# Gated attention mix: projection products split into two 64-row halves that run beside the scores

## The chip, the cores and the metric

The kernel runs on one core of a Trainium2 chip. The metric is device time in microseconds (us), from the start to the end of the program on that core. TensorE appears as PE in the profile (PEld is its weight load), VectorE as DVE, ScalarE as ACT, GpSimd as POOL, SyncE as SP. A bank is one of the eight PSUM areas of 128x512 float32 into which PE writes and from which ACT and DVE read.

## The reference, cut to what matters

Two attention blocks A and B share the input x of 2048x640 and differ in their weights. Their results are mixed row by row with a gate.

```python
def block(x, wqkv, wo):                       # S=2048, D=640, H=32 heads of Dh=20
    qkv = (x @ wqkv).reshape(B, S, 3, H, Dh).transpose(2, 0, 3, 1, 4)
    q, k, v = qkv
    p = softmax(einsum("bhqd,bhkd->bhqk", q, k) * Dh ** -0.5)
    o = einsum("bhqk,bhkd->bhqd", p, v)
    return o.transpose(0, 2, 1, 3).reshape(B, S, D) @ wo

g = sigmoid((x * gate_w).sum(-1, keepdims=True))
out = g * block(x, A_wqkv, A_wo) + (1 - g) * block(x, B_wqkv, B_wo)
```

## The kernel before

The heads are taken four at a time: 8 groups of block A, then 8 of block B, so 16 groups, numbered 0 to 15. In a group the 2048 queries go in four blocks of 512, and the 2048 keys in eight pairs of tiles of 128. One **step** is one query block against two key tiles for four heads; there are 16 x 4 x 8 = 512 steps (`STEPS`). Every matrix product of float32 data is done as three float16 products of a high and a low part (`wh`, `wl`, `xh`, `xl`).

What PE does in a step:

- **Scores** (`scores`, line 632): 8 matmuls of 64 rows by 512 columns. Head pairs sit in rows 0 to 63 (`j` = 0, in the order `e0`) and 64 to 127 (`e1`), so two scores of different halves run side by side. ACT takes each score's exponential out of its bank (line 635).
- **Maxima** (`max_mm`, line 574): 8 matmuls of the same size, transposed (`m0`, `m1`), for a query block to come, up to `LEAD` = 15 steps ahead. DVE reduces them to row maxima (line 585); for some, ACT first takes a Relu of one bank (line 578) and DVE joins it with a second (line 582). The scores of a query block can only start when its maxima are done, since the maximum is an operand row of the score.
- **Values** (`values`, line 650): twice a step four float32 matmuls of 128 rows, one per head, into the bank `acc` in strips of 32 columns. The order calls them `V`.
- **Products** (`mms`, line 375), called `X`: pieces of the projections of later groups (`project_a`, `project_r`: queries and keys; `project_v`: values), of the output projection (`out_tiles`) and of its last part (`last_tiles`, line 813). A piece is mostly 15 matmuls of 128 rows and 160 to 176 columns into one bank, which ACT (lines 402, 530, 715) or DVE (line 717) then takes out.

There are seven banks for scores, maxima and products. `take` gives the bank that is expected to be free first, `give` says when, with a clock kept at build time (`clock`, `rows_free`, `free_at`). On each engine the instructions run in the order in which the build writes them.

The order of a step is a text, picked by how late the products are: `STEP[0]` without a product, `STEP[1]` with one, `STEP[2]` with two, and `LATE` where no maxima are left. Products wait in the list `fill` with the step from which they may be done and the step by which they are due; `behind` compares the two, `slot` does one piece. Where a query block's maxima are not ready when its step comes, a loop does further maxima and pieces until they are. After the last step a second loop finishes what is left.

Of the kernel before, what the change touches and what calls it, by code (L numbers as in the profile page):

```python
# [31 lines left out]
NS = 8  # L32
# [29 lines left out]
def kernel(  # L62
# [73 lines left out]

    def tick_score(j, i):
# [230 lines left out]
    def mms(i, out_ap, pairs, cost):  # L368

        if now[0] >= 0:  # L370
            tick_block(len(pairs) * cost * T_SCORE, free_at[i])
        for k, (a, b) in enumerate(pairs):
            if now[0] < 0:
                tick_block(cost * T_SCORE, free_at[i])
            nc.tensor.matmul(out_ap, a, b, start=(k == 0), stop=(k == len(pairs) - 1))  # L375
            if now[0] < 0:
                yield
# [6 lines left out]
    def project_chunk(w, hi, lo, ch):  # L384
# [9 lines left out]
        if now[0] >= 0:  # L394
            f = work.tile([P, QB], F32, name="fs")
            for k in range(3):
                if k:
                    yield
# [4 lines left out]
                give(i, spend("act", 0.25, clock["done"]))  # L403
# [115 lines left out]
    def project_v(gg, j):  # L519
# [3 lines left out]
        for u in range(2):  # L523
            if u and now[0] >= 0:
                yield
            n = slice((j + u) * P, (j + u + 1) * P)
            i, pt = take()
            yield from mms(i, pt[:, :w], [(a[:, c, n], b[:, c, :w]) for c in range(NC) for a, b in
                                          ((xh, wh), (xh, wl), (xl, wh))], 0.33)
# [155 lines left out]
    def out_tiles(job, t, state):  # L685
# [17 lines left out]
        def products():  # L703
            wh, wl = wo_parts[z]
            for k in range(0, D, width):
                if k:
                    yield
                n = slice(k, k + width)
                i, pt = take()
                yield from mms(i, pt[:, :width], [(o[:p, a, c - c0], w[:p, c, n])  # L710
                                                  for c in range(c0, c1) for p in (P if c < full else 48,)
                                                  for a, w in ((0, wh), (0, wl), (1, wh))], width / QB)
# [17 lines left out]
        soon(state["due"], D // width, products())  # L730
# [71 lines left out]
    def last_tiles(qb, o):  # L802
        wh, wl = wo_parts[2]
        for t in range(4):
            c = slice(t * P, (t + 1) * P)
            f = f_o[1][:, 4 * qb + t:4 * qb + t + 1]
            for half in range(2):
                n = slice(half * 320, half * 320 + 320)
                y = y_sum[:, 4 * qb + t, n]
                i, pt = take()  # L810
                tick_block(0.4, free_at[i])
                for k, (a, w) in enumerate(((0, wh), (0, wl), (1, wh))):
                    nc.tensor.matmul(pt[:, :320], o[:, a, c], w[:, n], start=(k == 0), stop=(k == 2))  # L813
# [9 lines left out]
            yield  # L823
# [160 lines left out]
    for g in range(2 * NG):  # L984
        b = g * NQ * NS
        n = g + 1
        if n < 2 * NG:
            fill += [(b - 8, b + 4 + ch, 3, project_a(n, ch)) for ch in range(4)]
# [3 lines left out]
            if i < 4:  # L992
# [7 lines left out]
                if g % 4 == 3:  # L1000
                    fill += [(b - 9, b + 4 + ch, 3, project_r(i, ch)) for ch in range(4)]
            gg = g // 2 + 1
            if gg < NG and g % 2 == 0:
# [4 lines left out]
                fill += [(b + 10, b + 14 + 3 * j, 2, project_v(gg, j)) for j in range(0, NT, 2)]  # L1008
# [13 lines left out]
    outs = [(NG * step + 2 + int(9 * t), jobs[0], t) for t in range(NT)]  # L1022
# [9 lines left out]
    def out_tasks(G):  # L1032
# [8 lines left out]
        if last and all(4 * last[0][0] + t in summed for t in range(4)):  # L1041
            soon(now[0] + 6, 4, last_tiles(*last.pop(0)))

    def behind(G):

        n = sum(f[0] for f in current)
        for f in sorted((f for f in fill if f[0] <= G), key=lambda f: f[1]):
            n += f[2]
            if n > max(1, f[1] - G):
                return True  # L1050
        return False

    def slot(G):
        if not current:
            able = [f for f in fill if f[0] <= G]
            if not able:
                return
            first = min(able, key=lambda f: f[1])
            fill.remove(first)
            current.append([first[2], first[3]])  # L1060
        try:
            next(current[0][1])
            current[0][0] -= 1
        except StopIteration:
            current.clear()
# [37 lines left out]
    for G in range(STEPS + 1):  # L1103
        g, qb, i = unit_of(G)
        now[0] = G
        while G < STEPS and ((g, qb) not in ready or (G and not valued(G - 1))):
            for u, ch in next_maxima(G, 1):
                for j in (1, 0):
                    one_max(u, ch, j)
# [3 lines left out]
            slot(G)  # L1113
        some = next_maxima(G, 4)
        blocks = 0 if not current and not any(f[0] <= G for f in fill) else 2 if behind(G) else 1
        count = {}
        for what in (STEP[blocks] if maxima or some else LATE + " X" * (blocks == 2)).split():
            k = count[what] = count.get(what, 0) + 1
            if what[0] == "e":
                q = sum(count.get(f"e{j}", 0) for j in range(2)) - 1  # L1120
                j = int(what[1])
                if G < STEPS:
                    scores(G, (k - 1) // 2, (k - 1) % 2, (j,))
# [6 lines left out]
            elif what[0] == "m":  # L1130
                for u, ch in some[(k - 1) * len(some) // 4:k * len(some) // 4]:
                    one_max(u, ch, int(what[1]))
            elif what == "V":
                product()
                if G:
                    values(G - 1, k - 1)
                    if G % NS == 0 and k == 2 and G < STEPS:
                        side.append(take_acc(*unit_of(G - 1)[:2]))
                        advance()
            else:  # L1140
                slot(G)
# [35 lines left out]
```

## Time and profile before

| | |
|---|---|
| Time, median of 3 runs (lowest to highest) | 2835.39 us (2834.82 to 2835.52) |
| Span of the profiled execution, first to last instruction | 2832.8 us |
| Time around the span (median less span) | 2.6 us |
| PE, DVE, ACT busy | 2773.1, 2443.8, 2529.7 us |
| PE's granted clock, mean | 0.996 |
| Chain that ended last, share of PE | 91% |

The profiled execution has no time of its own beside its span, so the median of the runs less the span stands for what lies around it. Matmuls are recorded from start to the arrival of their result, so two that follow each other overlap in the records: how long a matmul keeps PE is read from the distance between two starts.

### The profile page before, as it was taken

The page shows a single profiled execution, that of the slowest core. Times are in us where ns is not written, and L with a number is a line of the kernel's source. Part 1 is how long each engine was busy: PE and PEld are TensorE (multiplying, and loading weights), DVE is VectorE, ACT ScalarE, POOL GpSimd, SP SyncE. Part 2 cuts the span into 40 slices and gives each one's busy share as a digit, 9 for nine tenths or more (in the row PEclk, how much of TensorE's full clock was granted, in tenths as well). Part 3 has the DMA queues.
Part 4 walks back from the last instruction along what each step waited for, and adds up shares of the span by engine and source line. Part 5 has one row for each costly group of instructions (what it writes and reads, how often), then busy time and mean ns, then how long its engine had stood idle before and what let it go on. Part 6 is the DMA issues. An engine that isn't in the chain of part 4 may idle for free.

```text
span 2832.8 us, 62443 instructions
## 1 busy us (share of the span) xinstructions
PE 2773.1 (98%) x23362; PEld 970.8 (34%) x23362; DVE 2443.8 (86%) x4763; ACT 2529.7 (89%) x5122; POOL 671.8 (24%) x914
## 2 busy tenths in 40 slices
PE   6999999999999999999999999999999999999998
PEld 3533223342323323343233333334333333332222
DVE  6688999879999898988989888887888989989982
ACT  3799999989999999989999999998899999888887
POOL 5312113231221212233431111222112233120011
PEclk9999999999999999999999999999999999999999
DMA  4110101001020101202021020211202112122222
GB/s 135 35 45 7 39 6 42 16 16 29 13 52 16 37 11 27 47 13 50 17 56 44 14 60 16 48 37 24 49 15 61 38 38 70 55 71 60 63 60 74
DMA packets 167170, 113.71 MB, mean 40 GB/s; under 512 B 102224, under 2 KB 140808, under 8 KB 166864
## 3 DMA queue, kind: packets, MB, share of 16 engines
q1 hardware_dynamic: 164320, 108.09, 15.6%
q8 instruction: 183, 3.00, 0.4%
q0 software_dynamic: 1600, 0.96, 0.2%
q14 instruction: 123, 1.01, 0.1%
q10 hardware_dynamic: 944, 0.66, 0.1%
HBM read 48.89 MB, written 26.61 MB: 27 GB/s over the span
## 4 chain that ended last, share of the span: by engine, by line
PE 91%; DVE 5%; ACT 1%; DMA 1%; POOL 1%; issue 1%; SPq 0%; POOLq 0%; DVEq 0%; ACTq 0%
PE acc L650 34%; PE bank L375 20%; PE bank L632 19%; PE bank L574 17%; DVE mpart L585 3%; ACT pt L635 1%; DVE rl L582 1%; DMA xs<-in_A_x_dram 0%; ACT rl L578 0%; DMA wv<-in_A_wqkv_dram 0%; DVE ot L736 0%; PE bank L813 0%; PE bank L183 0%; PE bank L862 0%; DVE wmax L227 0%
## 5 line engine op out<-in xcount | busy, mean ns | idle before, releaser
L635 ACT ACTIVATE pt<-bank 128x512 f32<-128x512 f32 x4096 | 2157.5, 614 | 155.0 <-PE bank L632 75.1
L585 DVE TENSOR_REDUCE mpart<-bank 128x1 f32<-128x512 f32 x2976 | 1867.8, 681 | 264.3 <-PE bank L574 167.1
L650 PE MATMUL acc<-pt,v 128*21 128x512 f32 x8192 | 1082.0, 600 | 3.4 <-DVE ot L736 3.1
L632 PE MATMUL bank<-qt,kt 64*128 64x512 f16 x4096 | 1056.3, 380 | 11.9 <-ACT pt L635 4.5
L574 PE MATMUL bank<-kt,qt 60*128 60x512 f16 x3536 | 1013.0, 380 | 4.0 <-DVE mpart L585 0.7
L574 PEld LDWEIGHTS <-qt 60*128 60x128 f16 x4096 | 235.4, 94 | 686.6 <-issue 629.0
L632 PEld LDWEIGHTS <-kt 64*128 64x128 f16 x4096 | 248.1, 94 | 456.7 <-issue 322.8
L582 DVE CUSTOM_DVE_ANT_0 rl<-bank,rl 128x512 f32<-128x512 f32 x560 | 377.5, 678 | 20.5 <-ACT rl L578 8.2
L578 ACT ACTIVATE rl<-bank 128x512 f32<-128x512 f32 x560 | 329.8, 595 | 14.6 <-PE bank L574 12.3
L744 POOL TENSOR_TENSOR ot<-ot,sq 128x512 f32<-128x512 f32 x63 | 66.0, 1047 | 993.0 <-DVE sq L741 993.0
L650 PEld LDWEIGHTS acc<-pt,v 128*21 128x21 f32 x8192 | 143.0, 99 | 434.6 <-issue 421.5
L375 PE MATMUL bank<-xx,wbh 128*128 128x168 f16 (+2 forms) x2240 | 280.1, 244 | 3.2 <-ACT xx L866 1.9
L375 PE MATMUL bank<-xx,wbl 128*128 128x168 f16 (+2 forms) x1120 | 252.8, 243 | 0.0
L375 PEld LDWEIGHTS <-wbh 128*128 128x128 f16 x2240 | 183.6, 98 | 86.8 <-issue 79.8
L574 PE MATMUL bank<-kd,qt 60*128 60x512 f16 x560 | 203.6, 381 | 1.7 <-DMA kd<-dd 1.2
L375 PE MATMUL bank<-wvh,xx 128*128 128x160 f16 (+1 forms) x1280 | 155.4, 234 | 0.5 <-ACT pt L635 0.3
L375 PE MATMUL bank<-woh,o_in 128*128 128x160 f16 (+1 forms) x960 | 155.7, 256 | 0.0
L375 PEld LDWEIGHTS <-xx 128*128 128x128 f16 x1920 | 131.6, 97 | 52.7 <-issue 49.4
L404 POOL CAST cq<-fs 128x512 f16<-128x512 f32 x60 | 36.6, 609 | 446.0 <-ACT fs L402 444.0
L375 PE MATMUL bank<-wvl,xx 128*128 128x160 f16 (+1 forms) x640 | 137.3, 231 | 0.6 <-POOL wvl L315 0.6
L375 PEld LDWEIGHTS <-o_in 128*128 128x128 f16 (+1 forms) x1440 | 104.0, 97 | 75.3 <-issue 62.2
L402 ACT ACTIVATE fs<-bank 128x168 f32<-128x168 f32 (+1 forms) x216 | 67.5, 313 | 56.6 <-PE bank L375 40.0
(131 smaller groups left out, 1305.2 us busy)
## 6 DMA issues: line engine op xcount, KB each, us to landing
y_scr<-y_out SPq DMA_DIRECT2D x32, 320.0 KB
kt<-cq SPq DMA_DIRECT2D x120, 80.0 KB
o_scr<-on SPq DMA_DIRECT2D x240, 40.0 KB
kt<-cq SPq DMA_DIRECT2D x136, 40.0 KB
xs<-in_A_x_dram SPq DMA_DIRECT2D x8, 640.0 KB
o_in<-o_scr SPq DMA_DIRECT2D x32, 160.0 KB
y_out<-y_scr SPq DMA_DIRECT2D x16, 320.0 KB
xx<-y_scr SPq DMA_DIRECT2D x16, 320.0 KB
```

The costliest lines, as they stand in the source:

```text
L375: nc.tensor.matmul(out_ap, a, b, start=(k == 0), stop=(k == len(pairs) - 1))
L402: nc.scalar.activation(f[:, m], pt[:, m], AF.Copy, scale=QKS)
L404: nc.gpsimd.tensor_copy(hi, f)
L574: nc.tensor.matmul(pt, QT[g % 2][r, pair, q0:q0 + P], k, start=True, stop=True)
L578: nc.scalar.activation(relus[u, j], pt, AF.Relu)
L582: nc.vector.tensor_tensor_reduce(rl, pt, rl, 1.0, LOW, OP.add, OP.max, m)
L585: nc.vector.tensor_reduce(m, pt, axis=AX.X, op=OP.max)
L632: nc.tensor.matmul(et, KT[g % 2][r, pair, kt * P:(kt + 1) * P], QT[g % 2][r, pair, qb * QB:(qb + 1) * QB], start=True, stop=True)
L635: nc.scalar.activation(pt, et, AF.Exp, scale=factor(g // 4))
L650: nc.tensor.matmul(acc[32 * h:32 * h + VW, :], V[(g // 2) % 2][:, kt, (g % 2) * GH + h, :], ptiles.pop((G, kk, h)), start=(kt == 0), stop= ...
L744: nc.gpsimd.tensor_tensor(t3, t3, sq.unsqueeze(2).to_broadcast([P, 16, 32]), op=OP.mult)
```

## The change

Products are no longer blocks of 128-row matmuls. `halves_of` writes each matmul as two of 64 rows: first all those on rows 0 to 63, then all those on rows 64 to 127, accumulating in the same bank. While a half runs on one set of rows, the scores and maxima of the other rows are written between its matmuls. The second half of a product may begin only when a wait that PE has already made proves that the first half's writes have landed (`seen`, `synced`, `wrote`); up to two products may be open at once (`limit=2`).

The order of a step is no longer a text. A loop writes scores and maxima in turn, and half matmuls where `wanted` allows them. `pace` sets how much product time a step may take, between `PACE` = 1.9 and `HASTE` = 3.4 us counted for one half (the old order could do two whole pieces). The values stand where 6/16 and 14/16 of the step's scores and maxima have been written. In the waiting loop and after the last step, `alone` does up to 15 products a turn as 128-row blocks (`solo`). The output tiles of the first job come every 6.2 steps instead of every 9.

```diff
-STEP = ("e0 m1 V e1 m0 e0 m1 e1 m0 e0 m1 e1 m0 V e0 m1 e1 m0",
-        "X e0 m1 m0 e1 m0 m1 V m1 e0 e1 m0 e1 e0 V m0 e1 e0 m1",
-        "X m0 m1 e0 m1 e0 e1 V e1 e0 m1 m0 V e1 m0 m1 m0 e0 e1 X")
-LATE = "e0 e1 e0 e1 V X e0 e1 e0 e1 V"
+COLUMN = 1 / 2400
+CHUNK = 30 * QB * COLUMN
+PACE, HASTE = 1.9, 3.4
...
+    def halves_of(width, pairs):
+        todo = [(r, slice(64 * r, min(64 * r + 64, a.shape[0])), a, b) for r in range(2) for a, b in pairs
+                if a.shape[0] > 64 * r]
+        cost = width * COLUMN + 0.003
+        i = pt = None
+        for k, (r, rows, a, b) in enumerate(todo):
+            turned = k > 0 and todo[k - 1][0] != r
+            yield r, cost, len(todo) * cost if k == 0 else 0, count[0] if turned else 0
+            if k == 0:
+                i, pt = take()
+                seen(i)
+                if solo[0]:
...
+                    return i, pt
...
+            nc.tensor.matmul(pt[:, :width], a[rows], b[rows], start=(k == 0), stop=(k == len(todo) - 1))
...
-            for k in range(3):
-                if k:
-                    yield
+            for k in range(len(PARTS) - 1):
                 m = slice(PARTS[k], PARTS[k + 1])
-                i, pt = take()
-                yield from mms(i, pt[:, m], pairs(slice(t0 + m.start, t0 + m.stop)), 0.34)
-                nc.scalar.activation(f[:, m], pt[:, m], AF.Copy, scale=QKS)
+                n = m.stop - m.start
+                i, pt = yield from halves_of(n, pairs(slice(t0 + m.start, t0 + m.stop)))
+                nc.scalar.activation(f[:, m], pt[:, :n], AF.Copy, scale=QKS)
...
-    outs = [(NG * step + 2 + int(9 * t), jobs[0], t) for t in range(NT)]
+    outs = [(NG * step + 2 + int(6.2 * t) + (45 if t > 12 else 0), jobs[0], t) for t in range(NT)]
...
+    def pace(G):
+        n, most = float(len(current)), PACE
+        for f in sorted((f for f in fill if f[0] <= G), key=lambda f: f[1]):
+            n += f[2]
+            most = max(most, 1.1 * n / max(1, f[1] - G))
+        return min(most, HASTE)
+
+    def wanted(G, limit=2, free=False):
+        for x in current:
+            if x[1][3] <= synced[0] and (x[1][2] == 0 or free or credit[0] > 0.0):
+                return x
+        while len(current) < limit and (free or credit[0] > 0.0):
...
         while G < STEPS and ((g, qb) not in ready or (G and not valued(G - 1))):
...
-            slot(G)
+            for _ in range(15):
+                alone(G)
...
+        v_at = [6 * total // 16, 14 * total // 16] if maxima or some else [total // 2, total]
...
+            r = x[1][0]
...
+            if not emit_s(1 - r):
+                emit_s(r)
+                continue
+            while True:
+                x = wanted(G)
+                if x is None or x[1][0] != r or rows_free[r] + 0.5 * x[1][1] > rows_free[1 - r]:
+                    break
+                emit_x(x)
```

**A step in the middle, on PE.** First the order before, from one `V` (line 650) to the next. L574 is a maximum, L632 a score, L375 a product's matmul; `bank0` to `bank6` are the seven banks, and "waits" names the engine whose reading of that bank must have ended.

```order
L650 MATMUL acc_88<-pt_15398,v1_87 21x512
L574 LDWEIGHTS qt1_81
L574 MATMUL bank6_95<-kt1_83,qt1_81 128x512 [waits DVE_49]
...
L632 MATMUL bank3_92<-qt0_80,kt0_82 128x512 [waits Activation_49]
...
L632 MATMUL bank4_93<-qt0_80,kt0_82 128x512 [waits DVE_49]
L574 LDWEIGHTS qt1_81
L574 MATMUL bank0_89<-kt1_83,qt1_81 128x512 [waits Activation_49]
L375 LDWEIGHTS xx_79
L375 MATMUL bank1_90<-wvh_14700,xx_79 128x160 [waits DVE_49]
...
L632 LDWEIGHTS kt0_82
L632 MATMUL bank5_94<-qt0_80,kt0_82 128x512 [waits Activation_49]
```

The product's 15 matmuls stand together, with four scores and maxima between the values and the product. Now the same stretch after the change, again from one values block to the next (L666 is a score, L608 a maximum, L410 a half matmul, L684 the values); between the rows shown stand three L410 matmuls each time, all into `bank1`.

```order
L684 MATMUL acc_88<-pt_18882,v1_87 21x512
L666 LDWEIGHTS kt1_83
L666 MATMUL bank4_93<-qt1_81,kt1_83 128x512 [waits DVE_49]
...
L608 MATMUL bank2_91<-kt1_83,qt1_81 128x512 [waits Activation_49]
...
L666 MATMUL bank0_89<-qt1_81,kt1_83 128x512 [waits Activation_49]
...
L608 MATMUL bank3_92<-kd1_85,qt1_81 128x512 [waits DVE_49]
...
L666 MATMUL bank6_95<-qt1_81,kt1_83 128x512 [waits DVE_49]
...
L608 MATMUL bank4_93<-kt1_83,qt1_81 128x512 [waits Activation_49]
...
L666 MATMUL bank0_89<-qt1_81,kt1_83 128x512 [waits Activation_49]
...
L608 MATMUL bank2_91<-kt1_83,qt1_81 128x512 [waits DVE_49]
...
L410 MATMUL bank3_92<-xx_79,wbh_17719 128x176 [waits Activation_49]
L684 MATMUL acc_88<-pt_18907,v1_87 21x512
```

Eight scores and maxima now stand between two values blocks, and `bank4`, `bank0` and `bank2` are each written twice within the stretch, while `bank1` and `bank5` hold open products. The first three rows are all on rows 0 to 63; the product's matmuls are on rows 64 to 127.

**The end of group 11, on PE.** Before the change the maxima of group 12 (L574, `qt0`) stand among the scores of group 11 (L632, `qt1`) throughout:

```order
L574 LDWEIGHTS qt0_80
L574 MATMUL bank2_91<-kt0_82,qt0_80 128x512 [waits DVE_49]
L632 LDWEIGHTS kt1_83
L632 MATMUL bank1_90<-qt1_81,kt1_83 128x512 [waits Activation_49]
L632 LDWEIGHTS kt1_83
L632 MATMUL bank4_93<-qt1_81,kt1_83 128x512 [waits DVE_49]
L574 LDWEIGHTS qt0_80
L574 MATMUL bank5_94<-kt0_82,qt0_80 128x512 [waits Activation_49]
```

After the change the last 13 steps of the group hold no maximum, and at its last step the waiting loop writes two 1-column matmuls (L1133), 30 half matmuls, then 315 product matmuls in one piece (L402, here its end), then the maxima of group 12 (L608):

```order
L402 MATMUL bank5_94<-wol_19690,o_in_32472 128x160
L402 LDWEIGHTS o_in_32472
L402 MATMUL bank5_94<-woh_19689,o_in_32472 128x160
L608 LDWEIGHTS qt0_80
L608 MATMUL bank6_95<-kd0_84,qt0_80 128x512 [waits Activation_49]
L608 LDWEIGHTS qt0_80 [waits DMAHW4_49,DMAHW3_49]
L608 MATMUL bank0_89<-kt0_82,qt0_80 128x512 [waits Activation_49]
```

In that place 95 maxima follow each other before the next score.

**After the last values block, on PE.** Before the change the four small L777 to L788 steps are followed by the last 24 matmuls of `last_tiles` (L813). After it, 129 further 320-column matmuls (L402) of output tiles that the steps had not reached stand between the two.

More of the change, by code (lines that the diff above doesn't have):

```diff
@@ L1058, in slot, with follow @@
             first = min(able, key=lambda f: f[1])
             fill.remove(first)
[L1060 to L1065, printed above, removed]
+            x = [first[3], None]
+            if follow(x):
+                return x
+        return None
+    def follow(x):
+        x[1] = next(x[0], None)
+        if x[1] is None:
+            if x in current:
+                current.remove(x)
+            return False
+        if x not in current:
+            current.append(x)
+        return True
@@ new lines, in emit_x, with alone @@
+    def emit_x(x):
+        credit[0] -= x[1][2]
+        follow(x)
+    def alone(G):
+        x = wanted(G, 1, True)
+        if x is None and current:
+            i, pt = take()
+            mark = wts.tile([P, 1], F32, name="m1", tag="m1", bufs=2)
+            for n in range(2):
+                tick_block(0.1, free_at[i])
+                seen(i)
+                nc.tensor.matmul(pt[:, :1], KT[1][:, 0, :P], KT[1][:, 0, :1], start=True, stop=True)
+                if n == 0:
+                    nc.vector.tensor_copy(mark, pt[:, :1])
+                    free_at[i] = spend("dve", 0.1, clock["done"])
+            give(i, clock["done"])
+        elif x is not None:
+            solo[0] = True
+            emit_x(x)
+            solo[0] = False
@@ L1145 @@
         product()
-        slot(STEPS)
+        for _ in range(15):
+            alone(STEPS)
         out_tasks(STEPS)
```

150 lines of the change are left out of this document (94 added, 56 removed).

## The prediction

> **What bounds the kernel now.** I read the page's head and its chain of waits first.
>
> ```profile
> span 2832.8 us, 62443 instructions
> PE 2773.1 (98%) x23362; PEld 970.8 (34%) x23362; DVE 2443.8 (86%) x4763; ACT 2529.7 (89%) x5122; POOL 671.8 (24%) x914
> PE 91%; DVE 5%; ACT 1%; DMA 1%; POOL 1%; issue 1%; SPq 0%; POOLq 0%; DVEq 0%; ACTq 0%
> ```
>
> PE sets the end, but ACT and DVE are close behind, so what a step costs depends on its mix. The timeline of PE shows a step with one product:
>
> ```profile
> 1441.50 1.06 PE L650 MATMUL acc<-pt,v 128*21 128x512 f32 x8
> 1442.49 0.39 PE L574 MATMUL bank<-kt,qt 60*128 60x512 f16 x1
> 1442.49 0.60 PE L632 MATMUL bank<-qt,kt 64*128 64x512 f16 x2
> 1442.72 0.38 PE L574 MATMUL bank<-kt,qt 60*128 60x512 f16 x1
> 1443.03 0.32 PE L375 MATMUL bank<-xx,wbh 128*128 128x168 f16 x2
> ...
> 1444.06 0.24 PE L375 MATMUL bank<-xx,wbl 128*128 128x168 f16 x1
> 1444.22 0.39 PE L632 MATMUL bank<-qt,kt 64*128 64x512 f16 x1
> ...
> 1448.26 0.32 PE L375 MATMUL bank<-xx,wbh 128*128 128x168 f16 x2
> ```
>
> Starts are what count. A pair of scores comes every 0.22 us; the product's 15 matmuls every 0.073 us (1443.03 to 1444.06 is 14 of them). Where PE goes between 64-row scores, 128-row products and the values, time is lost: 1442.72 + 0.22 is 1442.94, yet the product starts at 1443.03 (0.09), and 1444.06 + 0.07 is 1444.13, yet the next score starts at 1444.22 (0.09). The values cost 0.99 us to the next start. The step, product to product, is 5.23 us, with PE always working. A step without a product looks otherwise:
>
> ```profile
> 353.20 1.06 PE L650 MATMUL acc<-pt,v 128*21 128x512 f32 x8
> ...
> 354.95 1.06 PE L650 MATMUL acc<-pt,v 128*21 128x512 f32 x8
> ...
> 356.60 0.38 PE L632 MATMUL bank<-qt,kt 64*128 64x512 f16 x1
> 357.01 0.37 PE L574 MATMUL bank<-kt,qt 60*128 60x512 f16 x1
> 357.36 0.37 PE L632 MATMUL bank<-qt,kt 64*128 64x512 f16 x1
> 357.50 0.37 PE L574 MATMUL bank<-kt,qt 60*128 60x512 f16 x1
> 357.80 1.06 PE L650 MATMUL acc<-pt,v 128*21 128x512 f32 x8
> ```
>
> It takes 4.60 us (353.20 to 357.80). After seven scores PE's starts lie 0.41, 0.35 and 0.14 us apart on single matmuls: all seven banks are full and PE waits for ACT and DVE. How fast a bank comes back is seen elsewhere, with ACT idle before it:
>
> ```profile
> 709.84 0.39 PE L632 MATMUL bank<-qt,kt 64*128 64x512 f16 x1
> ...
> 710.26 0.60 ACT L635 ACTIVATE pt<-bank 128x512 f32<-128x512 f32 x1 [0.33 <-PE bank L574]
> ...
> 710.91 0.37 PE L632 MATMUL bank<-qt,kt 64*128 64x512 f16 x1 [0.24 <-ACT pt L635]
> ...
> 710.92 0.39 PE L574 MATMUL bank<-kt,qt 60*128 60x512 f16 x1
> ```
>
> From a score's start to the next score in its bank pass 1.07 us at the least: 0.4 until ACT begins, 0.6 for the exponential, the rest until PE goes on. The score at 710.92, for the other rows, stands behind the waiting one and starts after it.
>
> ```profile
> L635 ACT ACTIVATE pt<-bank 128x512 f32<-128x512 f32 x4096 | 2157.5, 614 | 155.0 <-PE bank L632 75.1
> L585 DVE TENSOR_REDUCE mpart<-bank 128x1 f32<-128x512 f32 x2976 | 1867.8, 681 | 264.3 <-PE bank L574 167.1
> L632 PE MATMUL bank<-qt,kt 64*128 64x512 f16 x4096 | 1056.3, 380 | 11.9 <-ACT pt L635 4.5
> ```
>
> A reduce is 0.07 longer than an exponential, so I take 1.15 us behind a reduce. Over the whole kernel PE sits idle before scores for 11.9 us only.
>
> **The change part by part.** The steps are measured between these two values blocks, 511 steps apart: 2706 us.
>
> ```profile
> 106.10 1.06 PE L650 MATMUL acc<-pt,v 128*21 128x512 f32 x8
> ...
> 2812.24 1.06 PE L650 MATMUL acc<-pt,v 128*21 128x512 f32 x8
> ```
>
> I add up each built order with these durations (a column at 1/2400 us and 2.5 ns a matmul, which gives 0.216 and 0.0725; each half's rows in turn, in the order written, both free before the values). Without any wait PE needs 2549 us before and 2580 after, +31:
>
> - **Mode changes.** They fall from 2883 to 2072: 811 x 0.093 = -75. The half matmuls cost no more rows x columns than the whole ones, so nothing else is saved.
> - **Idle halves.** Before the values both halves must be done. Summed over the stretches between values, the busier half has 1438 us and the mean of both 1329: 109 us of half the array idle (before: 7). Scores left for one half only, after the other half's were spent beside a product, make it. Written order adds 21 more (before 4). Together +119.
> - 13 us of products move out behind the last step: -13.
>
> **Banks** are the large term. A product held its bank for its 1.2 us block and the taking out; now it holds it for about ten scores and one or two values, and two can be open. A score finds its bank's last score 5.5 scores back on average instead of 6.6, and there are no blocks in which banks come back. Take the stretch shown after the change: three scores on the same rows at 0, 0.22 and 0.43, then one every 0.22 us, so `bank0` is wanted again at 1.30. Its first exponential waits for that of `bank4` and the bank is free at about 0.86 + 0.69 = 1.55: PE stands 0.25 us. Over the order, with 1.07 and 1.15 as the least return, 1178 scores wait in 861 of the 1022 stretches, and the sum grows by 244; before, 222 scores wait in 117 stretches, all without a product, and it grows by 58. Net +186. It is least: queues of ACT and DVE come on top, and what stands in the same rows behind the score waits too. Bounds: 0 (banks keep up) and +265 (returns as in the worked stretch, another 0.08 a stretch).
>
> Part of this hides where ACT or DVE set the step anyway:
>
> ```profile
> 2808.59 4.03 ACT L635 ACTIVATE pt<-bank 128x512 f32<-128x512 f32 x8 [0.38 <-PE bank L632]
> 336.07 3.61 DVE L585 TENSOR_REDUCE mpart<-bank 128x1 f32<-128x512 f32 x6
> ```
>
> Eight exponentials take 3.95 us, a reduce 0.59 (0.53 per maximum, as one in eight has only a Relu); with 0.45 of small work a step of eight maxima takes DVE 4.65, against 4.60 seen. Raising each step to these floors lifts the sum before to 2645 and after to 2841: -21 against the sums of PE. The 61 us by which 2706 exceeds 2645 (small work on DVE, rounding) I carry over unchanged. Steps: +196.
>
> The Trainium skill, TensorEngine Tiling (Array Packing), "Restrictions and Gotchas", says that row tiling increases PSUM pressure, and that tiles on different rows may not use one bank at once. The returns above agree with the first; with it the sum is the forecast, without it the second case below. TensorE: Matmul & The Clock Gate, "Part 3", says matmuls start strictly in program order; 710.91 and 710.92 agree, so half matmuls behind a waiting score are no cover, and if they could pass it the bank term would shrink towards 0.
>
> **End of group 11.** 315 product matmuls (23 us) come first, with ACT and DVE all but empty, then 95 maxima at DVE's 0.53 (50 us). The floor counts only the longer of the two: +25. What covered the maxima before were the 13 steps that now have none.
>
> **The end.** 129 matmuls of 320 columns now follow the last values:
>
> ```profile
> 2784.61 1.00 SPq L694 DMA_DIRECT2D o_in<-o_scr  x1
> ...
> 2785.55 0.31 PE L375 MATMUL bank<-woh,o_in 128*128 128x320 f16 x1
> ...
> 2785.70 0.30 PE L375 MATMUL bank<-wol,o_in 128*128 128x320 f16 x1
> ...
> 2785.84 0.54 PE L375 MATMUL bank<-woh,o_in 128*128 128x320 f16 x2
> ...
> 2786.59 0.43 SPq L697 DMA_DIRECT2D xx<-y_scr  x1
> kt<-cq POOLq DMA_DIRECT2D x16, 20.0 KB, 1.9
> ```
>
> At 0.14 each they are 18 us. The last tile's loads stand on SP behind four output stores that wait for DVE; issue (2784.61 to 2787.02) and a landing of about 2 us leave some 4 us open. +22; bounds 0, if it ran beside the closing chain, and 30.
>
> ACT's and DVE's work is unchanged in number; POOL's follows the products and hides behind 76% idle time.
>
> **Sum:** 2832.8 + 196 + 25 + 22 = 3075.8; with the 2.6 us around the span, by which the median of 2835.39 exceeds it, **3078 us**.
>
> **The rivals.** A measurement tells 0.2% (6 us) from no change.
>
> - **Banks bind** (forecast, 60%): 3078; own range 2985 (half the bank term) to 3160.
> - **Banks keep up** (18%): ACT and DVE, fed more evenly, return banks before they are asked for. The steps then go by idle halves and floors alone, 2662 against 2643: 2835.4 + 19 + 25 + 22 = 2901. For it: 11.9 us of idle time before scores now. Against: 1.07 us is the least seen, and the order asks for less.
> - **Queues compound** (12%): exponentials and reduces queue behind each other as in the worked stretch, 0.08 us more in 1022 stretches: 3160, and up to 3200 with stores.
> - **Even products win** (faster, 6%): a product-free step leaves PE idle for 0.7 us (4.60 less two values at 1.08 and eight pairs at 0.22), and two products in a step leave ACT and DVE idle; product time spread evenly fills both. If no bank is waited for and the 23 us of the waiting loop hide, the floors sum to 2639 against 2645, and the 61 us of left-over waits can go: 2835.4 - 6 - 61 + 22 = 2790. It decides as soon as banks return within 0.87 us, four scores at 0.22.
> - **No change** (2%): gains of that kind meet the tail.
> - **Halves don't overlap** (2%): if a 64-row product matmul held up the other half's scores, 446 us of halves would come twice: about 3500. Against: the two scores at 1442.49, one of each half, start together.
>
> **How the numbers follow.** The likeliest case gives 3078. The range 2880 to 3195 holds that case, most of the second and most of the third, 80%. Faster 6%, same 2%, slower 92%.
>
> **What would show it.** After the change, steps near 5.6 us in groups 8 to 14; PE's idle time before scores (11.9 now), ended by ACT and DVE, above 80 us; ACT and DVE busy shares down to 82 and 79%; in the slices three quarters through, DVE alone for 50 us; 20 us more behind the last values. If scores keep 0.22 us apart between half matmuls, the bank term is wrong and the second case holds; if a half matmul starts while a score waits, the order rule is.

## The result, and the profile after

The changed kernel takes **3158.07 us** (median of four runs, 3156.48 to 3159.16), the kernel before on the same chip 2835.11 us: a ratio of 1.114 (95% interval 1.113 to 1.116), 11.4% slower. The forecast was 3078, with a range of 2880 to 3195. Direction and range held; the added time is 323 us where 243 was forecast.

The page's head after the change, and its time slices for PE, DVE, ACT and PE's clock:

```profile
span 3155.1 us, 73952 instructions
PE 3007.8 (95%) x29298; PEld 1285.6 (41%) x29298; DVE 2476.4 (78%) x4764; ACT 2503.1 (79%) x5122; POOL 671.0 (21%) x914
PE   6999999999999999999999999999999999999998
DVE  6788888778887888877888777777529888888873
ACT  4788888888888888888888878777854888888885
PEclk9999999999999999999999999999987999999999
```

ACT and DVE have as much to do as before (2503 and 2476 us busy, before 2530 and 2444), spread over a longer span: 79 and 78% instead of 89 and 86%. Something between PE and them has become slower. Two dents are seen in the slices: DVE falls to 5 and 2 three quarters through, and PE's clock to 8 and 7 at about the same place.

The span has three parts. The values blocks mark them; of each kernel this is the row of the view of one line, with the first and the last start near its end. Before:

```profile
L650 PE MATMUL acc<-pt,v x8192: 592/600/610, 106.1 to 2814.7; 128*21 128x512 f32 x200
```

After:

```profile
L684 PE MATMUL acc<-pt,v x8192: 592/607/1061, 104.5 to 3113.6; 128*21 128x512 f32 x200
```

From first to last they grow from 2708.6 to 3009.1 us, +300.5. Ahead of the first 1.6 us are saved, and behind the last stand 41.5 us where 18.1 stood, +23.4. Together 322.3, the difference of the spans.

**What PE could do by itself, and what it did.** For each of the 1023 stretches from one values block to the next I add up what PE needs when it waits for nothing: values 0.892 us, a column at 1/2400 us and 2.5 ns a matmul, 0.0925 us a mode change (a turn between 64-row matmuls, 128-row products and values), and the busier half of the rows between two turns. All but the last are read from starts in these two traces: 0.216 us from one matmul to the next on the same rows for 512 columns, 0.136 for 320 and 0.073 for 168, 0.99 from a values block to the matmul behind it (values and one turn), and 0.086 to 0.097 left over at a turn. Against this sum I set the traced distance between the two values blocks. The rest is waiting; the sum takes PE's clock as full and leaves out the order in which the two halves are written, so what these cost is in the rest too. All in us:

| | values | both halves, mean | idle half | whole products | mode changes | own sum | beyond it | stretches |
|---|---|---|---|---|---|---|---|---|
| before | 912.5 | 880.8 | 7.3 | 480.5 | 266.3 | 2547.3 | 160.8 | 2708.2 |
| after | 912.5 | 1323.4 | 108.9 | 23.3 | 191.7 | 2559.9 | 448.4 | 3008.3 |

PE's own work is 13 us longer after the change: the mode changes saved (-75) and the products moved out (-15) are eaten by idle halves (+102). The loss is in the last step: 288 us more of waiting. Two stretches at the end of group 11 hold 47 of them (38.2 and 8.5), the other 241 lie all over the kernel: 933 stretches of 1023 wait more than 0.05 us, before 456. Values blocks, which need the exponentials, wait for less than 2 us of it in all; the rest stands before matmuls that need a bank, and before half matmuls written behind them.

The costliest groups show this badly:

```profile
L669 ACT ACTIVATE pt<-bank 128x512 f32<-128x512 f32 x4096 | 2193.1, 622 | 487.6 <-PE bank L608 227.5
L619 DVE TENSOR_REDUCE mpart<-bank 128x1 f32<-128x512 f32 x2976 | 1901.3, 682 | 413.8 <-PE bank L608 259.3
L666 PE MATMUL bank<-qt,kt 64*128 64x512 f16 x4096 | 1340.6, 379 | 32.4 <-ACT pt L669 10.1
L608 PE MATMUL bank<-kt,qt 60*128 60x512 f16 x3536 | 1250.2, 382 | 58.9 <-ACT pt L669 11.1
L608 PE MATMUL bank<-kd,qt 60*128 60x512 f16 x560 | 207.5, 382 | 12.5 <-DVE mpart L616 4.6
```

ACT now sits idle for 488 us before exponentials (155 before), but PE shows only 32 us of idle time before scores and 71 before maxima. A matmul is recorded until its result arrives, 0.38 us for one that keeps its rows for 0.216; a wait of up to 0.16 us (0.38 less 0.216) leaves no gap in the records, and one on one half of the rows is covered by a matmul on the other. Starts must be read, not gaps.

### The profile page after: what moved, and what is told of

Read it like the earlier page. It is cut to its first block, busy times and chain, and to the rows that moved or that the text cites. A ratio compares the mean times of both kernels' runs of the same rounds, so it can differ in the third digit from the quotient of the medians.

```text
span 3155.1 us, 73952 instructions
## 1 busy us (share of the span) xinstructions
PE 3007.8 (95%) x29298; PEld 1285.6 (41%) x29298; DVE 2476.4 (78%) x4764; ACT 2503.1 (79%) x5122; POOL 671.0 (21%) x914
## 5 line engine op out<-in xcount | busy, mean ns | idle before, releaser
L666 PE MATMUL bank<-qt,kt 64*128 64x512 f16 x4096 | 1340.6, 379 | 32.4 <-ACT pt L669 10.1
L608 PE MATMUL bank<-kt,qt 60*128 60x512 f16 x3536 | 1250.2, 382 | 58.9 <-ACT pt L669 11.1
L684 PE MATMUL acc<-pt,v 128*21 128x512 f32 x8192 | 1084.5, 601 | 0.0
L666 PEld LDWEIGHTS <-kt 64*128 64x128 f16 x4096 | 328.9, 94 | 747.9 <-issue 704.3
L410 PE MATMUL bank<-xx,wbh 64*128 64x168 f16 (+1 forms) x4080 | 562.6, 236 | 5.2 <-ACT rl L612 2.2
L608 PEld LDWEIGHTS <-qt 60*128 60x128 f16 x4096 | 347.1, 94 | 373.0 <-issue 309.6
L410 PE MATMUL bank<-xx,wbl 64*128 64x168 f16 (+1 forms) x2040 | 462.7, 234 | 0.0
L410 PEld LDWEIGHTS <-wbh 64*128 64x128 f16 x4080 | 311.6, 94 | 155.4 <-issue 112.7
L410 PE MATMUL bank<-wvh,xx 64*128 64x160 f16 x2140 | 308.9, 231 | 0.7
L410 PE MATMUL bank<-woh,o_in 64*128 64x160 f16 (+2 forms) x1692 | 295.5, 251 | 1.3 <-DVE mpart L616 0.2
L684 PEld LDWEIGHTS acc<-pt,v 128*21 128x21 f32 x8192 | 143.4, 99 | 296.5 <-issue 224.0
L410 PEld LDWEIGHTS <-xx 64*128 64x128 f16 x3210 | 220.5, 94 | 101.1 <-issue 68.2
L410 PE MATMUL bank<-wvl,xx 64*128 64x160 f16 x1070 | 237.5, 229 | 0.0
L608 PE MATMUL bank<-kd,qt 60*128 60x512 f16 x560 | 207.5, 382 | 12.5 <-DVE mpart L616 4.6
L410 PEld LDWEIGHTS <-o_in 64*128 64x128 f16 (+1 forms) x2538 | 177.1, 94 | 98.3 <-issue 62.6
L410 PE MATMUL bank<-wol,o_in 64*128 64x160 f16 (+2 forms) x846 | 204.9, 250 | 0.0
L410 PEld LDWEIGHTS <-wbl 64*128 64x128 f16 x2040 | 191.6, 94 | 18.4 <-issue 10.5
```

Source lines behind the costliest of these rows:

```text
L410: nc.tensor.matmul(pt[:, :width], a[rows], b[rows], start=(k == 0), stop=(k == len(todo) - 1))
L608: nc.tensor.matmul(pt, QT[g % 2][r, pair, q0:q0 + P], k, start=True, stop=True)
L666: nc.tensor.matmul(et, KT[g % 2][r, pair, kt * P:(kt + 1) * P], QT[g % 2][r, pair, qb * QB:(qb + 1) * QB], start=True, stop=True)
L684: nc.tensor.matmul(acc[32 * h:32 * h + VW, :], V[(g // 2) % 2][:, kt, (g % 2) * GH + h, :], ptiles.pop((G, kk, h)), start=(kt == 0), stop= ...
```

## What the experiments showed

In each, "beyond" is the waiting of the table above, worked out from that kernel's own trace in the same way.

### Is it the halves, or the order around them?

**whole.** The changed loop with every product as one 128-row block.

```diff
-    solo = [False]
+    solo = [True]
...
-            solo[0] = False
+            solo[0] = True
```

> The changed kernel's loop, but every product is again one block of 128-row matmuls; nothing is written in halves. By its order PE needs 2625 us between the values blocks (values 912, scores and maxima 881, idle halves 73, products 479, mode changes 279), against 2560 in the changed kernel and 2547 in the one before. What was measured beyond such a sum is 448 us in the changed kernel and 161 before. Banks held by open half products (my forecast): the waits fall back to about 161, total 2625 + 161 + 127 outside = about 2915. Rival, the order: eight scores and maxima in a row between values blocks are what fills the banks, whoever does the products; then the waits stay near 400 and the total is about 3150. A mixture would lie between.

Measured: 3077.23 us, 1.086 of before (1.083 to 1.089). The mixture: own sum 2624.6, beyond 323. So with no product in halves, 162 of the 288 us are there. They sit in 597 stretches that hold eight scores and maxima and no product, 0.465 us each, 278 us together. On PE:

```profile
1440.50 1.06 PE L684 MATMUL acc<-pt,v 128*21 128x512 f32 x8
1441.49 0.39 PE L608 MATMUL bank<-kt,qt 60*128 60x512 f16 x1
1441.50 0.39 PE L666 MATMUL bank<-qt,kt 64*128 64x512 f16 x1
1441.72 0.38 PE L608 MATMUL bank<-kt,qt 60*128 60x512 f16 x1
1441.72 0.38 PE L666 MATMUL bank<-qt,kt 64*128 64x512 f16 x1
1441.93 0.38 PE L608 MATMUL bank<-kt,qt 60*128 60x512 f16 x1
1441.94 0.59 PE L666 MATMUL bank<-qt,kt 64*128 64x512 f16 x2
1442.60 0.37 PE L608 MATMUL bank<-kt,qt 60*128 60x512 f16 x1
1442.90 0.63 PE L684 MATMUL acc<-pt,v 128*21 128x512 f32 x4
```

Three pairs come 0.22 us apart and fill six banks, the seventh goes to a score at 1442.15 (the second of the two in the row at 1441.94), and the eighth matmul starts at 1442.60, 0.45 us after its rows were free. A run of six in the kernel before has no such gap:

```profile
1519.72 1.06 PE L650 MATMUL acc<-pt,v 128*21 128x512 f32 x8
1520.71 0.39 PE L574 MATMUL bank<-kt,qt 60*128 60x512 f16 x1
1520.71 0.60 PE L632 MATMUL bank<-qt,kt 64*128 64x512 f16 x2
1520.94 0.38 PE L574 MATMUL bank<-kt,qt 60*128 60x512 f16 x1
1521.16 0.38 PE L632 MATMUL bank<-qt,kt 64*128 64x512 f16 x2
1521.47 1.06 PE L650 MATMUL acc<-pt,v 128*21 128x512 f32 x8
```

In the kernel before 425 runs of six wait 0.053 us each on average, and 95 runs of ten 0.729.

**order8.** The kernel before, with one values block moved by two places.

```diff
-        "X e0 m1 m0 e1 m0 m1 V m1 e0 e1 m0 e1 e0 V m0 e1 e0 m1",
+        "X e0 m1 m0 e1 V m0 m1 m1 e0 e1 m0 e1 e0 V m0 e1 e0 m1",
```

> The kernel before, with one letter of the order of a one-product step moved: its first values block stands two places earlier, so that eight scores and maxima follow each other between the two values blocks where six did. PE's own sum stays 2547; 342 runs of eight take the place of runs of six. Order (a run longer than seven banks can hold waits): with the means of the whole-block run and of the kernel before (0.47 us in a run of eight, 0.05 in one of six) + 0.42 x 342 = + 144, about 2975. Rival, only banks held by open products matter, of which this kernel has none more than before: 2835, at most 2860.

Measured: 2987.64 us, 1.054 (1.051 to 1.057). One letter costs 153 us. PE's own sum is the same to the tenth; beyond rises from 161 to 315, of which 171 lie in 324 runs of eight (0.53 each). One of them on PE:

```profile
1505.81 1.06 PE L650 MATMUL acc<-pt,v 128*21 128x512 f32 x8
1506.80 0.39 PE L574 MATMUL bank<-kt,qt 60*128 60x512 f16 x2
1507.02 0.38 PE L632 MATMUL bank<-qt,kt 64*128 64x512 f16 x1
1507.03 0.38 PE L574 MATMUL bank<-kt,qt 60*128 60x512 f16 x1
1507.24 0.38 PE L632 MATMUL bank<-qt,kt 64*128 64x512 f16 x1
1507.24 0.38 PE L574 MATMUL bank<-kt,qt 60*128 60x512 f16 x1
1507.46 0.88 PE L632 MATMUL bank<-qt,kt 64*128 64x512 f16 x2
1508.27 0.63 PE L650 MATMUL acc<-pt,v 128*21 128x512 f32 x4
```

Seven start by 1507.46; the eighth, the second in the row at 1507.46, starts at 1507.97, 0.51 us after its rows were free. This is the clearest single result of the study: with the same banks and the same work on every engine, the longer run of scores and maxima alone costs half as much as the whole change did.

**whole_6.** The reverse: runs of six and ten in the loop with whole products.

```diff
-        v_at = [6 * total // 16, 14 * total // 16] if maxima or some else [total // 2, total]
+        v_at = [6 * total // 16, 12 * total // 16] if maxima or some else [total // 2, total]
```

> The changed kernel's loop with whole products, and its second values block at 12/16 of the step's scores and maxima instead of 14/16: the runs between values alternate six and ten, with the product in the longer one. PE's own sum is 2624, as with whole products before. Order: 645 runs of six, 117 of ten and 480 with a product, at 0.05, 0.73 and 0.08 us, make about 160 us of waits where 323 were; about 2915. Rival, the loop itself (the way in which it turns between the halves) is what costs: it stays within 30 us of 3077.

Measured: 2978.28 us, 1.051 (1.048 to 1.054), 99 us below the whole-block run. The direction is that of the order, but only 99 of the 163 us went (beyond 225). The 483 runs of six cost 0.035 us each, as thought; 114 runs of ten cost 0.90 instead of 0.73, and 105 stretches of six, a product and four cost 0.37 where I had put 0.08, and no run tells why.

### How much is a bank worth?

**six_before** and **six_after.** One bank is never given out after the start.

```diff
     start_stack.close()
+    held.add(6)
```

> The kernel before, with one of its seven banks never given out after the start: six banks, all else by the same rules. An open product holds a bank for 9.8 us on average after the change, 1.32 banks at any time, against 0.17 before; this kernel has 0.15 bank more to give than the changed one. Banks alone: nearly all of the 287 us of added waits come back, + 250, about 3085. Rival, the order: a bank less costs little where products stand as blocks, + 0 to 60, at most 2895. A mixture: + 140, about 2975.

> The changed kernel, with one of its seven banks never given out after the start. Open products hold 1.26 banks on average over the scores, so 4.7 are left for the scores instead of 5.7; in the kernel before, the step from 7 to 6 cost 148 us. Banks: a step from 5.7 to 4.7 costs more than that, + 150 to + 300, about 3380; the stall at the end of group 11 is gone from the order (no whole products are left inside), which takes back 40. Rival, the waits come from runs of scores alone: + 30 to + 100, about 3220.

Measured: 2983.30 us, 1.053 (1.050 to 1.056), +148 for the kernel before, beyond 309; a run of six then waits 0.16 us instead of 0.05. For the changed kernel 3413.37 us, 1.204 (1.201 to 1.208), +255, beyond 710. Its order has no block of whole products at the end of group 11 and so not that stall; against the other 401 us of waits its 710 are 309 more. The same bank is worth about twice as much after the change, which fits open products that already hold 1.26 banks there. Banks alone would have put the first at 3085, so they are not the only cause either.

**short_before** and **short_after.** Exponentials, Relus and maxima read half a bank only; these kernels leave out the other half of that work. Their main lines:

```diff
-            nc.scalar.activation(pt, et, AF.Exp, scale=factor(g // 4))
+            nc.scalar.activation(pt, et[:, :HB], AF.Exp, scale=factor(g // 4))
...
-                nc.vector.tensor_reduce(m, pt, axis=AX.X, op=OP.max)
+                nc.vector.tensor_reduce(m, pt[:, :HB], axis=AX.X, op=OP.max)
```

> The kernel before, with exponentials, Relus and maxima that read only 256 of a bank's 512 columns (the values read the 256 exponentials twice); half of that work is left out, PE's is unchanged. If the 161 us beyond PE's own sum of 2547 are waits for banks, most go: steps 2560 to 2600, total 2685 to 2730. If they are something of PE's own, the total stays above 2800.

> The changed kernel, with exponentials, Relus and maxima that read only 256 of a bank's 512 columns; half of that work is left out, PE's is unchanged. Banks (whoever fills them): the waits nearly vanish, and it ends above the kernel before with the same cut by the terms that are PE's own, 13 us between the values blocks, about 20 for the stretch at the end of group 11 and 24 behind the last values, so 60 us in all (40 to 110). Rival: half matmuls hold PE up by themselves (their issue, their weight loads, or scores that can't pass them); then the two stay 250 us or more apart.

Measured: 2751.64 us, 0.971 (0.968 to 0.974), and 2859.13 us, 1.009 (1.006 to 1.012). Beyond falls from 161 to 81 and from 448 to 154. These are the head and the costliest ACT and PE groups of the changed kernel so cut:

```profile
PE 2801.1 (98%) x29298; PEld 1281.4 (45%) x29298; DVE 1636.1 (57%) x4764; ACT 1620.3 (57%) x5122; POOL 672.2 (24%) x914
L670 ACT ACTIVATE pt<-bank 128x256 f32<-128x256 f32 x4096 | 1416.2, 388 | 1078.3 <-PE bank L609 492.9
L667 PE MATMUL bank<-qt,kt 64*128 64x512 f16 x4096 | 1316.0, 379 | 5.9 <-ACT pt L670 1.3
```

An exponential takes 0.39 us instead of 0.62, and 299 us go, with the same 29298 matmuls on PE. The two kernels end 107 us apart, not 250 or more, so most of the loss is not something that half matmuls do to PE by themselves. 107 is the upper end of what I had expected, since 154 us of waits remain, 19 of them in one stretch at the end of group 11. These two runs can't tell banks that come back late from ACT and DVE that have too much to do in a step; order8 and six_before, with the same work on both engines as before, can, and point to the banks.

### How long half products hold their banks

**dense22** and **dense15.** Half matmuls may run ahead of the other rows by 0.22 or 0.15 us, so that a product is done sooner.

```diff
-                if x is None or x[1][0] != r or rows_free[r] + 0.5 * x[1][1] > rows_free[1 - r]:
+                if x is None or x[1][0] != r or rows_free[r] + 0.5 * x[1][1] > rows_free[1 - r] + 0.22:
```

> The changed kernel, with half matmuls written until their rows are 0.22 us ahead of the other rows, not level with them: a half product is done beside fewer scores. Its price by the order: 227 us of idle halves instead of 109, PE's own sum 2689 instead of 2560. Open products hold 0.74 banks instead of 1.26, no stretch of whole products is left at the end of group 11, and 8 us of products instead of 18 remain for the end. Banks held: half a bank at 150 to 300 us a bank is - 75 to - 150, the stall - 47, the end - 13, idle halves + 118: 3060 to 3140, faster than the change. Rival, PE's own sum decides: + 129 - 60, about 3225, slower than the change.

> The changed kernel, with half matmuls written until their rows are 0.15 us ahead of the other rows (0 in the change, 0.22 in the run before this one, which took 3009 us). By the order 107 us of idle halves (109 and 227), PE's own sum 2567 (2560 and 2689), 0.86 banks held by open products (1.26 and 0.74), no stall at the end of group 11, 12 us of products left for the end. Banks: the waits lie between the 192 us of the 0.22 run and the 402 us (without the stall) of the change, by the banks held about 240; 2567 + 240 + 135 outside = about 2945, the fastest with halves. Rival, it was the idle time itself that gave ACT and DVE room: then what is saved in idle halves comes back as waits, 192 + 120 = 312, about 3010.

Measured: 3009.27 us, 1.062 (1.058 to 1.065), and 3009.83 us, 1.062 (1.060 to 1.064). Both are 148 us below the change, more than I had expected of the first, and less of the second:

| | banks held by open products (from the order) | idle half | beyond | idle half + beyond |
|---|---|---|---|---|
| change | 1.26 | 108.9 | 448.4 | 557.3 (47 of it at the end of group 11) |
| 0.15 us ahead | 0.86 | 107.5 | 310.0 | 417.5 |
| 0.22 us ahead | 0.74 | 226.6 | 192.3 | 418.9 |

From the change to 0.15 us the halves stay as idle and the waits shrink by 138: 47 of that is the stall, which neither of these orders has, and 91 go with the banks held. From 0.15 to 0.22 the waits shrink by what the idle halves grow. Time in which PE does nothing on one half is also time in which ACT and DVE give banks back, so in these two runs one takes the place of the other, as the rival had it. In the 0.22 run 109 of the 192 us are again in 224 runs of eight without a product.

### The end of group 11

**catch.** One whole product in a step whose backlog has reached the cap of the pace.

```diff
         credit[0] = max(min(credit[0], 1.0), -2.0) + rate
+        if rate == HASTE:
+            x = wanted(G, 3, True)
+            if x is not None and x[1][2] > 0:
+                solo[0] = True
+                emit_x(x)
+                solo[0] = False
+                credit[0] = max(credit[0], 1.0)
```

> The changed kernel, but in a step in which the backlog has driven the pace to its cap, one product is done as a whole block of 128-row matmuls. The 315 product matmuls and 95 maxima that follow each other at the end of group 11 are no longer there as one piece; half products as before elsewhere (1.23 banks held, idle halves 109, PE's own sum 2565). If that stall is worth the 47 us of waits read from the trace of the change: 3158 - 40, about 3115. Rival, the 25 us of the forecast: about 3135. Third, the work is only late elsewhere: within 8 us of 3158.

Measured: 3120.63 us, 1.101 (1.099 to 1.103), 37 us below the change. Group 11 took 209 us instead of 249. The trace of the change showed the stall as two pieces. On DVE:

```profile
2320.28 0.16 DVE L1135 COPY m<-bank 128x1 f32<-128x1 f32 x1 [26.12 <-PE bank L1133]
2346.03 1.29 DVE L619 TENSOR_REDUCE mpart<-bank 128x1 f32<-128x512 f32 x2 [25.59 <-PE bank L608]
```

By engine, with the stretch's length, PE, PEld, DVE, ACT and POOL, then PE's clock:

```profile
2350.00:2394.00 44.00, 41.28 (x85) 7.33 (x83) 43.86 (x86) 7.58 (x13) 0.83 (x3) 0.50 0.08 19
```

DVE had already been idle for 26 us in the steps without maxima. For another 25.6 us it waits while PE does whole products; then, to 2394, DVE is busy all the time (43.86 of 44.00 us) and PE waits for it, at a clock of 0.50.

### A version faster than both

**even8.** What the runs asked for is products as whole blocks, runs of at most six, and a product in as many steps as can be. The kernel before has the first, and the second in all steps but those without a product, whose written order has a run of ten. This moves only the due times of its products, so that fewer steps go without:

```diff
-            fill += [(b - 8, b + 4 + ch, 3, project_a(n, ch)) for ch in range(4)]
+            fill += [(b - 8, b + 12 + ch, 3, project_a(n, ch)) for ch in range(4)]
...
-                    fill += [(b - 9, b + 4 + ch, 3, project_r(i, ch)) for ch in range(4)]
+                    fill += [(b - 9, b + 12 + ch, 3, project_r(i, ch)) for ch in range(4)]
```

> The kernel before, with the queries' and keys' products due eight steps later, so that they are spread over more steps: by its order 398 steps with one product, 86 with none and 28 with two, where 343, 114 and 55 were. A step took 4.59 us with none, 5.34 with one, 6.44 with two: a pair of none and two costs 0.35 more than two with one. 27 such pairs: - 9.5, about 2826. Rival, the later products hold up a query block's maxima or scores: 2835 or more.

Measured: 2818.93 us (median of four runs), 0.9946 of before (0.9930 to 0.9963). It is faster than both kernels, if only by half a per cent of the one before: 15 us rather than 9.5. Beyond falls from 161 to 141, most of it because 70 runs of ten are left of 95 (69 to 51 us).

## Why the prediction was right, and where it was not

- **That banks bind, and the direction.** Right. Waiting is 288 of the 300 us between the values blocks, and it shrinks when banks come back sooner (short_after) or are held for less (dense15), and grows when there is one less (six_after).
- **Their size.** Here the 80 us are missing. Waits together with the end of group 11 were put at +190 (186 - 21 + 25) and are +288. The forecast sum was that of least returns: 1178 scores would wait. In the trace 1768 scores and maxima start over 0.05 us after their rows are free. Behind an exponential the median return of those is 1.14 us, near the 1.07 taken; behind a maximum it is 1.39, where 1.15 was taken, and a quarter of each is above 1.33 and 2.33. The prediction itself said that queues of ACT and DVE come on top, and then carried the 61 us left over from the kernel before unchanged. That is the step that failed. Between the two values blocks that were 2706 us apart before, the changed kernel took 3007 us; less the 2841 of its floors and the 25 for group 11 that leaves 141 where 61 were carried, and this is the missing 80. The size is that of the rival "queues compound" (3160), which had 12%; the return times speak for its mechanism, but no run singles it out.
- **The cause within it.** The prediction named two things in one sentence, that half products hold their banks and that blocks in which banks come back are gone. The runs separate them. The loop's runs of eight are enough for 162 us with no half product at all, and one letter in the old order makes 153. With halves the shares of the 448 us are different: 65 us in 127 runs of eight without a product, 47 in the stall, and 337 in the other stretches, nearly all with open half products. The two causes don't add up; that each takes slack which the other would need is my reading, and no run shows it.
- **Idle halves and mode changes.** +102 and -75, as worked out. Whether the further 17 us for the written order came can't be told, since they would stand among the 288; that rows don't always keep to it (below) speaks against it.
- **End of group 11.** It was put at 23 us of products and 50 of maxima (95, of which 92 stand ahead of the first score); the stretch from one values block to the next took 75.8 us, 2318.33 to 2394.18. That it costs 25 beyond the floors was a matter of how the floors were counted; taking it away saved 37.
- **The end.** +22 forecast, +23.4 measured, and so close in part by luck. The output tiles' matmuls took PE 26.4 us (3118.36 to 3144.75) where 18 and 4 for loads were put: PE stood only 1.6 us for the loads, but the first 7 us ran at half clock (below). The chain around them came 3 us shorter than before: 5.5 us instead of 7.0 from the last values to the next product's matmul, and 3.1 instead of 4.8 for the last 24 matmuls.
- **The signs.** Steps near 5.6 us in groups 8 to 14: 5.92 on average without group 11. ACT and DVE at 82 and 79%: 79 and 78%. DVE alone for 50 us: 48 (2346 to 2394). Idle time of PE before scores above 80 us: 32.4, or 104 with the maxima; the sign was badly chosen, since the records hide most of the waits. A half matmul that starts while a score waits: seen where the score waited for its rows, not where it waited for a bank (below), so the order rule held where the bank term needs it.
- **"Even products win"** fell for half matmuls, but evenness as such was worth something: spread over more steps as whole blocks, products save 15 us (even8).

## What to carry to other kernels

Count the banks against the longest run of matmuls that each need a fresh one: with seven banks runs of six cost 0.05 us here, of eight 0.47 to 0.53, and of ten 0.73, so two places in a written order were worth 5% of a kernel. Blocks that need no new bank, which look like lost time for the engines behind PE, are what lets the banks come back; filling them with work that holds a bank for some ten scores and as many maxima gives up part of the slack that banks need, and one bank was worth 148 us here. And where instructions overlap in the records, set the distance between starts against the work's own sum, since idle time showed 104 us of 448.

## What the runs showed of the hardware that I had not expected

**Rows pass each other, but not a waiting matmul.** In the written order the score below waits for ACT's reading of `bank0_89` and stands ahead of the half matmuls of the other rows:

```order
L666 MATMUL bank0_89<-qt1_81,kt1_83 128x512 [waits Activation_49]
L410 LDWEIGHTS wbh_7943
L410 MATMUL bank3_92<-xx_79,wbh_7943 128x176
...
L666 MATMUL bank6_95<-qt1_81,kt1_83 128x512 [waits DVE_49]
L608 LDWEIGHTS qt1_81
L608 MATMUL bank1_90<-kt1_83,qt1_81 128x512 [waits Activation_49]
L410 LDWEIGHTS wbh_7682
L410 MATMUL bank2_91<-xx_79,wbh_7682 128x176
```

On PE after the change:

```profile
714.23 0.38 PE L608 MATMUL bank<-kt,qt 60*128 60x512 f16 x1
714.26 0.24 PE L410 MATMUL bank<-xx,wbl 64*128 64x176 f16 x1
714.34 0.31 PE L410 MATMUL bank<-xx,wbh 64*128 64x176 f16 x2
714.45 0.38 PE L666 MATMUL bank<-qt,kt 64*128 64x512 f16 x1
...
714.67 0.38 PE L608 MATMUL bank<-kt,qt 60*128 60x512 f16 x1
714.73 0.24 PE L410 MATMUL bank<-xx,wbl 64*128 64x176 f16 x1
714.95 0.37 PE L666 MATMUL bank<-qt,kt 64*128 64x512 f16 x1
715.13 0.25 PE L410 MATMUL bank<-xx,wbh 64*128 64x176 f16 x1
715.17 0.38 PE L608 MATMUL bank<-kt,qt 60*128 60x512 f16 x1
```

The second half matmul of the row at 714.34 starts near 714.41 and is written behind the score at 714.45, which was held up by its own rows (714.23 + 0.22). At 715.13 a half matmul starts ahead of the maximum at 715.17, which is written before it and whose rows were again busy. But its own rows, 64 to 127, had been free since 714.89 (714.67 + 0.22): it came only when the two waiting instructions ahead of it had what they waited for. Some 1800 half-row matmuls of this trace start over 20 ns ahead of one written before them, 69 in the kernel before. The Trainium skill, TensorE: Matmul & The Clock Gate, "Part 3: Packing small matmuls", says that matmuls start and end strictly in program order; with two sets of rows loaded unevenly this trace doesn't agree, by 0.04 us in both places shown. For waits on semaphores the order held: in all but 35 of the 1800 places the matmul passed started within 0.05 us of when its own rows came free, so it had nothing else to wait for.

**PE's clock was half where PE had waited.** In the row 2350 to 2394 above, where PE waits for DVE, the granted clock is 0.50, and the values block behind it took 1.91 us instead of 1.06. Behind the last values, where PE had stood three times for 0.4 to 0.8 us, it is 0.51 for 7 us, and 320-column matmuls came 0.27 us apart instead of 0.14; the kernel before shows 0.52 in the same place (2818 to 2825). The values block on PE, and the stretches behind the last values by engine:

```profile
2394.18 1.91 PE L684 MATMUL acc<-pt,v 128*21 128x512 f32 x8
```

```profile
3118.00:3125.00 7.00, 7.00 (x29) 3.69 (x28) 5.00 (x12) 0.00 (x0) 0.00 (x0) 0.51 0.24 94
3125.00:3135.00 10.00, 9.50 (x59) 4.16 (x57) 4.96 (x11) 1.02 (x4) 1.58 (x4) 1.00 0.60 174
```

So the stall was paid for once more by what follows it; no run here separates what sets the clock. The Trainium skill, TensorE: Matmul & The Clock Gate, "Part 1: The HAM clock gate", gives two clock states in its table, half and full; the 0.50, 0.51 and 1.00 of these rows agree.
